# Turning tiles with both halves of TensorE's rows at once, two tensors to a pair of banks

## The chip, the cores and the metric

The kernel runs on one core of a Trainium2 chip. The metric is the device time of one execution in microseconds (us), the median of three executions: 617.34 us before the change (617.13 to 621.12).

## What is computed

Two blocks follow each other. The first is a linear recurrence over 768 tokens for 4 batches of 8 heads of width 40; the second is an MLP with a softmax-weighted activation and a layer norm.

```python
# r, k, v, w, a, b: (4, 8, 768, 40) float32
for t in range(S):
    y[:, :, t] = np.einsum('bhd,bhde->bhe', rt, state)
    Sa = np.einsum('bhde,bhe->bhd', state, at)
    state_decay = state * wt[:, :, None, :] - np.einsum('bhd,bhe->bhde', Sa, bt)
    state = state_decay + np.einsum('bhd,bhe->bhde', vt, kt)
# x = y as (3072, 320); w_in (320, 1024), w_out (1024, 320), g_ln (1024,), float64 in DRAM
h = x @ w_in
solu = h * softmax(h)
ln = (solu - mean(solu)) / np.sqrt(var(solu) + 1e-06) * g_ln
out = (ln @ w_out).astype(np.float32)
```

## The kernel before

The tokens are cut into 12 chunks of C = 64, and two batches share the 128 partitions: batch 0 of a pair in partitions 0 to 63, batch 1 in 64 to 127. That makes N = 24 units of work (2 batch pairs x 12 chunks). Within a chunk the recurrence is solved with small matrix products and the inverse of a 64x64 triangular matrix per head, so most products need the chunk's tensors with head width in the partitions and tokens along the free axis. The raw data lie the other way round (tokens in partitions), so each is turned by TensorE: `turned` (L347) takes a tensor of 128 partitions (two batches of 64 tokens) and 8 heads of 64 columns, and makes four transposes of 128 rows by 104 columns (two heads at a time), each into a quarter of one bank of PSUM. A copy of ScalarE (`kept`, L357) or a product on VectorE takes the bank into SBUF. Per unit these are turned: `ei` (the decay, L362, evicted into `ex`), `a` (`front`, L368, evicted by VectorE as `aT`), `b` (`front_b`, L376), `k` and `v` (`attend_kv`, L493), `r` (`attend_r`, L500), and the carried state `st` (`stated`, L505, evicted as `s`). In the MLP, `folded` (L711) turns the 128x1024 activation `e` with eight full 128x128 transposes, four to a bank, evicted as `lnT`.

The main loop (L823 to L901) is written out by hand: every engine runs its instructions in the order in which the program issues them. One pass of the loop is called a slot here. Slot i solves unit i of the recurrence, prepares units i+1 and i+2, runs the early steps for unit j = i + 5, and runs the MLP for units some three to four slots behind (m = i - 1; `hidden` L661, `highest`, `exped`, `weighed`, `folded`, `output` L723). `some` and `narrow` insert steps of two other lists on VectorE: the inversion of triangular blocks (`invert`, L423, 31 small steps per two units) and the conversion of the 64-bit weights.

PSUM has eight banks here: `ps1` is two buffers of a pair of banks (the small products rotate through them), `ps2` is one pair for the 128x1024 `h`, and `ps3` is two buffers of a single bank (`bank`, L142). All transposes, the cumulative sum of the decay (`pcum`, L333) and the output accumulator (`po`, L729) rotate through those two single banks.

TensorE is used with three shapes of the array. The small products use quarters (64 rows by 64 columns; four run at once, in four corners). The large products and the transposes use the full array. The third piece of the contraction of `h` has 64 rows only, and its two halves (L667 to L671, kt = 2) use the array's upper and lower half of rows, 64 rows by 128 columns each, each half writing its own bank; `fence` (L269) drains TensorE after it.

Of the kernel before, what the change touches and what calls it, by code (L numbers as in the profile page):

```python
# [17 lines left out]
P = 128  # L18
# [6 lines left out]
LAG = 1  # L25


THIN = (5, 15)
LN_EXP = "natural_log_exp_and_others"


# [20 lines left out]
def kernel(  # L52
# [33 lines left out]
    dram = ctx.enter_context(tc.tile_pool(name="dram", bufs=3, space=bass.MemoryType.DRAM))  # L86
    ps1 = ctx.enter_context(tc.tile_pool(name="ps1", bufs=2, space=PSUM))
    ps2 = ctx.enter_context(tc.tile_pool(name="ps2", bufs=1, space=PSUM))
    ps3 = ctx.enter_context(tc.tile_pool(name="ps3", bufs=2, space=PSUM))
    ctx.enter_context(tc.manual_schedule(engines={mybir.EngineType.PE, mybir.EngineType.Pool, mybir.EngineType.DVE,  # L90
                                                 mybir.EngineType.SP, mybir.EngineType.Activation}))

# [46 lines left out]
    def banks(name):  # L139
        return ps1.tile([P, 2, 512], FP32, tag="banks", name=name)  # L140

    def bank(name):  # L142
        return ps3.tile([P, 512], FP32, tag="bank", name=name)

# [71 lines left out]
                land(LANDS_NEXT[load], nc.gpsimd)  # L218

    def turn_g():  # L220
        pg = bank("pg")
        nc.tensor.transpose(out=pg[:, 0:NF], in_=g_rows, identity=ident[0:NF, 0:NF])
        for x, y in zip(g_cols, (0, -20, -36)):
            nc.scalar.mul(out=x, in_=pg[:, 0:NF], mul=2.0 ** y)
# [4 lines left out]
            nc.tensor.matmul(t[:, 0:DM], lhsT=c_("mean"), rhs=w2[:, c, :], start=start and c == lo, stop=stop and c == hi - 1)  # L229

    def mean_of(lo, hi, begun):
        t = bank("pmean")
        nc.tensor.matmul(t[:, 0:DM], lhsT=ident, rhs=begun, start=True, stop=False)
        mean_part(t, lo, hi, False)
        return mean_kept(t)
# [55 lines left out]
    def ok(i):  # L291
        return 0 <= i < N
# [29 lines left out]
    def logged(i):  # L322
        lw = st[i]["lw"] = two.tile([P, DM], FP32, tag="lw", name="lw", bufs=1)
        nc.scalar.activation(out=lw, in_=st[i]["raw_w"].rearrange("p h d -> p (h d)"), func=AF.Ln)

    def decay(i):
        if not ok(i):
            return
        d = st[i]
        if "lw" not in d:  # L330
            logged(i)
        t = (bank("pcum") if i > 5 else ps2.tile([P, DFF], FP32, tag="h", name="h"))[:, 0:DM]
        nc.tensor.matmul(t, lhsT=c_("cum"), rhs=d["lw"], start=True, stop=True)  # L333
        nc.scalar.activation(out=ei_t[0][:, :, 0:D], in_=heads(t), func=AF.Exp)
        inv = d["inv"] = two.tile([P, DM], FP32, tag="inv", name="inv", bufs=4)
        nc.scalar.activation(out=inv, in_=t, func=AF.Exp, scale=-1.0)
# [7 lines left out]
            j = H * (n == "b")  # L344
            nc.gpsimd.tensor_tensor(out=kb[:, j:j + H, 0:D], in0=d["raw_" + n], in1=heads(d["inv"]), op=ALU.mult)

    def turned(name, x):  # L347
        t = bank("p" + name)
        for j in range(4):
            nc.tensor.transpose(out=t[0:W2, j * P:(j + 1) * P],  # L350
                                in_=x[:, 2 * j:2 * j + 2].rearrange("p a b -> p (a b)")[:, 0:W2], identity=ident)
        return t[0:W2].rearrange("p (j b t) -> p b j t", j=4, b=2)

    def tokens(name, bufs=1):
        return two.tile([P, 2, 4, C], FP32, tag=name, name=name, bufs=bufs)
# [1 line left out]
    def kept(name, t, bufs=1):  # L357
        o = tokens(name, bufs)
        nc.scalar.copy(out=o[0:W2], in_=t)
        return o  # L360

    def decay_turned(i):  # L362
        if not ok(i):
            return
        ex = st[i]["ex"] = ex_t[i % (AHEAD + 2)]
        nc.scalar.copy(out=ex[0:W2, :, :, 1:], in_=turned("ei", ei_t[0]))

    def front(i):  # L368
        if not ok(i):
            return  # L370
        d = st[i]
        t = turned("a", d["raw_a"])
        aT = d["aT"] = tokens("aT", AHEAD)
        nc.vector.tensor_tensor(out=aT[0:W2], in0=t, in1=d["ex"][0:W2, :, :, 0:C], op=ALU.mult)

    def front_b(i):  # L376
        if not ok(i):
            return
        d = st[i]
        d["bT"] = kept("bT", turned("b", d["kb"][:, H:]))  # L380

    def masked(dst, t):
        nc.vector.tensor_tensor(out=dst, in0=t.rearrange("p b (j c) -> p b j c", j=4),  # L383
# [109 lines left out]
    def attend_kv(i):  # L493
        if not ok(i):
            return
        d = st[i]
        d["kT"] = kept("kT", turned("k", d["kb"]))
        d["vT"] = kept("vT", turned("v", v_t[0]))

    def attend_r(i):  # L500
        if not ok(i):
            return
        st[i]["rT"] = kept("rT", turned("r", r_t[0]), 2)

    def stated(i):  # L505
        if not ok(i):
            return
        d = st[i]
        bp, ci = where_(i)
        if ci:  # L510
            t = bank("pst")
            for x in range(4):
                nc.tensor.transpose(out=t[0:W2, x * P:(x + 1) * P],  # L513
                                    in_=st_t[bp][:, 2 * x:2 * x + 2].rearrange("p a b -> p (a b)")[:, 0:W2], identity=ident)
            d["s"] = two.tile([P, 4, P], FP32, tag="s", name="s", bufs=1)
            nc.scalar.copy(out=d["s"][0:W2], in_=t[0:W2].rearrange("p (x t) -> p x t", x=4))

    def scores(i):
        if not ok(i):
# [141 lines left out]
    def hidden(i, some):  # L661

        if not ok(i):
            return
        d = st[i]
        for kt, x in some:
            if (kt, x) == (NK - 1, 0):  # L667
                d["h"] = ps2.tile([P, DFF], FP32, tag="h", name="h")
            part = slice(0, P) if kt < 2 else half(x)
            mm(d["h"][:, 512 * x:512 * x + 512], d["xT"][part, kt], w_in[part, 2 * kt + (x if kt < 2 else 0)],  # L670
               start=kt == NK - 1, stop=kt == NK - 2)  # L671
# [39 lines left out]
    def folded(i):  # L711
        if not ok(i):
            return
        d = st[i]
        lnT = d["lnT"] = two.tile([P, NF, P], FP32, tag="lnT", name="lnT", bufs=1)
        for x in range(2):
            t = bank("plnT")
            for j in range(NF // 2):
                f = x * (NF // 2) + j
                nc.tensor.transpose(out=t[:, j * P:(j + 1) * P], in_=d["e"][:, f * P:(f + 1) * P], identity=ident)  # L720
            nc.scalar.copy(out=lnT[:, x * (NF // 2):(x + 1) * (NF // 2)].rearrange("p f t -> p (f t)"), in_=t)  # L721

    def output(i, x):  # L723
        if not ok(i):
            return
        d = st[i]
        bp, ci = where_(i)
        if x == 0:
            d["out"] = bank("po")  # L729
        for f in range(x * NF // 2, x * NF // 2 + NF // 2):  # L730
            nc.tensor.matmul(d["out"][:, 0:DM], lhsT=d["lnT"][:, f, :], rhs=w2[:, f, :], start=f == 0, stop=f == NF - 1)  # L731
        if x == 0:
            return
        osb = two.tile([P, DM], FP32, tag="osb", name="osb", bufs=1)
        nc.scalar.activation(out=osb, in_=d["out"][:, 0:DM], func=AF.Copy, scale=d["rs"])  # L735
        nc.scalar.dma_start(out=out.rearrange("(b s) n -> b s n", b=B)[2 * bp:2 * bp + 2, ci * C:ci * C + C], in_=osb)
# [26 lines left out]
    load_keys(2, "ba")  # L763
    decay(0)
    logged(1)
    decay_turned(0)
    for i in range(4):
        if i != 2:
            scaled(i, "b")
        if i == 3:  # L770
            scaled(0, "k")
            scaled(1, "k")
        front(i)
        front_b(i)
        decay(i + 1)
        if i == 0:
            logged(i + 2)
        some(4 * (i > 2))
        norm(i)
        decay_turned(i + 1)  # L780
        if i == 1:
            load_keys(3, "w")
            scaled(2, "b")
            begin_inverse(0)
            narrow(2)
            load_keys(3, "ba")
            load_keys(0, "k")
            load_keys(4, "w")
            load_values(0)
            load_keys(1, "k")  # L790
            load_keys(4, "ba")
            load_keys(5, "w")
            land(2, nc.sync)
        if i == 2:
            some(12)
# [27 lines left out]
    for i in range(-1, N + 3 + LAG):  # L823
# [7 lines left out]
        narrow(0, pieces[0])  # L831

        solved(i)
        if i in THIN:
            stated(i)
            front(j)
        if i >= 0:
            scores(i + 1)
        if i >= 0:
            load_keys(j + 3, "w")  # L840
        load_keys(j + 2, "bak")

        if i not in THIN:
            stated(i)
            front(j)
        hidden(m - 2, ((0, 1),))
        if i == 3 + LAG:
            centred(mean)
        narrow(some_weights[1], pieces[1])
        front_b(j)  # L850
        if ok(j + 2):
            logged(j + 2)
        if i == 1 + LAG:
            first = ps2.tile([P, DFF], FP32, tag="h", name="mean")
            mean_part(first, 0, 2, True, False)
        decay_turned(j + 1)
        hidden(m - 2, ((1, 1),))
        flip(i + 1)
        highest(m - 2)
        scaled(j + 1)  # L860
        left(i - 1)
        if i == 1 + LAG:
            mean_part(first, 2, 3, False)
            mean = mean_kept(first)
        decay(j + 2)
        output(m - 3, 0)

        some(pieces[2])
        if i == 2 + LAG:
            mean = mean_of(3, 6, mean)  # L870
        couple(i + 1)
        exped(m - 2)
        norm(j)
        answered(i)
# [10 lines left out]
        carried(i + 1)  # L885
        narrow(some_weights[2], pieces[3], ok(j) and j % GRP == GRP - 1)
        by_value(i + 2)
        if ok(m - 1):
            hidden(m - 1, ((2, 0), (2, 1)))
        fence()  # L890
        read(i, False)
        driven(i + 1)
        leave(i)
        begin_narrow(narrowed.get(i + 1, (0,))[0])
        folded(m - 2)
        hidden(m - 1, ((0, 0),))
        attend_kv(i + 2)
        hidden(m - 1, ((1, 0),))
        attend_r(i + 2)
        if i == 2 + LAG:  # L900
# [31 lines left out]
```

## Time and profile before

| | us |
|---|---|
| three executions | 617.34, 617.13, 621.12 |
| the profiled execution, first to last instruction | 616.2 |
| TensorE busy (matmul) | 552.0 (90%) |
| VectorE busy | 449.0 (73%) |
| ScalarE busy | 265.8 (43%) |
| GpSimd busy | 258.0 (42%) |
| granted TensorE clock, mean | 0.928 |

All times below are from this one execution. The profile names an instruction by engine, line, operation and tiles (output <- inputs; for a matmul the moving operand first, then the stationary one). "128*104 128x128" is a matmul with 128 rows and 104 columns of weights and an output (for a transpose: a moving operand) of 128 columns. An ordinary float32 matmul leaves two records, a transpose one. Matmuls are pipelined: a record lasts from its start to the modelled end of its last row, so the time that a group takes on TensorE is read from the start of the group to the start of the next one, not from the sum of the records.

### The profile page before, as it was taken

Reading aid. Unit: us, or ns where it says so; the run is one execution under the profiler, and the core shown is the slowest. Engines: PE = TensorE matmul, PEld = TensorE weight load, DVE = VectorE, ACT = ScalarE, POOL = GpSimd, SP = SyncE. Lnnn points to the kernel's source line nnn. Section 1 sums busy time; section 2 is a strip of 40 time slices with the busy share of each in tenths; the row PEclk is TensorE's granted clock in tenths of the full one; section 3 lists DMA queues with packets and bytes.
Section 4 is the critical chain, followed back from the end, with each engine's and each line's share of the span. In section 5 each row is a group of like instructions: output and inputs, shape, how many; then the busy total and the mean of one; then the engine's idle time right before and its main releaser. Section 6 shows DMA issues by size and latency. Waiting matters only on the chain.

```text
span 616.2 us, 26656 instructions
## 1 busy us (share of the span) xinstructions
PE 552.0 (90%) x11453; PEld 401.9 (65%) x11453; DVE 449.0 (73%) x1262; ACT 265.8 (43%) x548; POOL 258.0 (42%) x424
## 2 busy tenths in 40 slices
PE   5555668889999999999999999999999999999994
PEld 3333457666676777777777777777777676676652
DVE  4797986988968869869868868788697588443431
ACT  3433444654543544454444445444433343342221
POOL 3463264283453472473365355444624631322200
PEclk9665765789999999999999999999999999999998
DMA  7986887476455455564564474564532622310100
GB/s 164 159 156 121 183 157 129 98 156 104 76 106 104 90 115 99 93 122 95 100 123 91 95 126 98 112 113 82 110 56 53 118 49 43 65 35 26 28 19 21
DMA packets 213901, 59.93 MB, mean 97 GB/s; under 512 B 199120, under 2 KB 208952, under 8 KB 213784
## 3 DMA queue, kind: packets, MB, share of 16 engines
q1 hardware_dynamic: 195512, 33.78, 32.8%
q0 software_dynamic: 11568, 19.78, 14.0%
q10 hardware_dynamic: 6704, 4.67, 2.7%
q8 instruction: 90, 1.47, 1.0%
q14 instruction: 27, 0.22, 0.1%
HBM read 40.10 MB, written 13.37 MB: 87 GB/s over the span
## 4 chain that ended last, share of the span: by engine, by line
PE 74%; DVE 17%; ACT 3%; issue 3%; DMA 1%; ACTq 1%; DVEq 0%; SPq 0%
PE po L731 16%; PE h L265 16%; PE pyo L265 8%; DVE uu L438 5%; DVE prod L436 5%; PE pu L265 4%; PE plnT L720 4%; PE ps L265 4%; PE px L265 3%; PE py L265 2%; PE pl L265 2%; PE pz L265 2%; PE pr L350 2%; PE pst L513 2%; PE pcum L333 1%
## 5 line engine op out<-in xcount | busy, mean ns | idle before, releaser
L265 PE MATMUL h<-w_in,xT 128*128 128x512 f32 (+1 forms) x288 | 123.7, 614 | 0.0
L731 PE MATMUL po<-w,lnT 128*128 128x320 f32 x384 | 112.7, 438 | 0.5 <-ACT lnT L721 0.5
L438 DVE TENSOR_TENSOR uu<-uu,prod 128x30 f32<-128x30 f32 (+4 forms) x360 | 102.1, 284 | 12.4
L436 DVE TENSOR_TENSOR prod<-blk,uu 128x30 f32<-128x30 f32 (+4 forms) x360 | 99.2, 276 | 9.6
L731 PEld LDWEIGHTS po<-w,lnT 128*128 128x128 f32 x384 | 71.0, 190 | 32.6 <-issue 4.1
L409 POOL DMA_DIRECT2D nt_dram<-nt x20 | 18.8, 938 | 120.8 <-DVE nt L383 99.8
L709 POOL TENSOR_TENSOR rs<-c,mhalf 128x1 f32<-128x1 f32 x24 | 13.5, 561 | 112.3 <-DVE c L708 103.4
L383 DVE TENSOR_TENSOR psi<-ps,cst 128x512 f32<-128x512 f32 x24 | 16.6, 690 | 59.5 <-PE ps L265 59.5
L658 POOL DMA_DIRECT2D xT<-x x96 | 48.9, 514 | 0.4 <-DMA blk<-nt_dram 0.3
L265 PEld LDWEIGHTS h<-w_in,xT 128*128 128x128 f32 (+1 forms) x288 | 37.6, 190 | 9.4 <-issue 8.1
L678 DVE TENSOR_REDUCE nmax<-h 128x1 f32<-128x1024 f32 x24 | 28.6, 1193 | 18.6 <-PE h L265 18.6
L420 POOL DMA_DIRECT2D blk<-nt_dram x46 | 36.9, 808 | 11.8 <-issue 8.4
L265 PE MATMUL pyo<-lv,kb 64*64 64x104 f32 x768 | 38.3, 269 | 2.2
L265 PEld LDWEIGHTS pyo<-lv,kb 64*64 64x64 f32 x768 | 24.1, 142 | 21.2 <-issue 21.1
L265 PE MATMUL pyo<-lu,kb 64*64 64x104 f32 x768 | 37.4, 262 | 0.1
L646 POOL TENSOR_TENSOR st<-tot,ex 104x160 f32<-104x160 f32 x44 | 21.7, 511 | 36.4 <-DVE tot L642 32.4
L562 ACT COPY x<-px 128x320 f32<-128x320 f32 x24 | 10.2, 426 | 56.3 <-PE px L265 56.1
L477 ACT ACTIVATE wy<-py,cst 128x256 f32<-128x256 f32 x24 | 11.4, 474 | 53.2 <-PE py L265 53.2
L288 POOL DMA_DIRECT2D raw_r<-in_r_dram x48 | 33.9, 709 | 0.0
L735 ACT ACTIVATE osb<-po,rs 128x320 f32<-128x320 f32 x24 | 12.7, 527 | 48.5 <-PE po L731 32.8
L686 ACT ACTIVATE e<-h,nmax 128x1024 f32<-128x1024 f32 x24 | 26.6, 1108 | 14.3 <-DVE nmax L678 14.3
L692 DVE TENSOR_TENSOR e<-h,e 128x1024 f32<-128x1024 f32 x24 | 29.2, 1217 | 4.7 <-ACT e L686 4.7
(131 smaller groups left out, 1169.1 us busy)
## 6 DMA issues: line engine op xcount, KB each, us to landing
blk<-nt_dram POOLq DMA_DIRECT2D x46, 128.0 KB, 4.7
nt_dram<-nt POOLq DMA_DIRECT2D x20, 256.0 KB, 3.7
raw_w<-in_w_dram SPq DMA_DIRECT2D x48, 80.0 KB
a<-in_a_dram SPq DMA_DIRECT2D x48, 80.0 KB
raw_r<-in_r_dram POOLq DMA_DIRECT2D x48, 80.0 KB, 3.6
lv<-in_v_dram SPq DMA_DIRECT2D x48, 80.0 KB
out_dram<-osb ACTq DMA_DIRECT2D x24, 160.0 KB
raw_b<-in_b_dram SPq DMA_DIRECT2D x44, 80.0 KB
```

Of the source, the lines that this page charges most:

```text
L265: nc.tensor.matmul(o, lhsT=lhsT, rhs=rhs, start=start, stop=stop, skip_group_check=True)
L288: queue.dma_start(out=x[half(p), :, 0:D], in_=ap[2 * bp + p, :, ci * C:(ci + 1) * C, :].rearrange("h t d -> t h d"))
L420: queue.dma_start(out=nb[home:home + Q], in_=blocks[n][:, Q * e:Q * e + Q, Q * e:Q * e + Q])
L436: nc.vector.tensor_tensor(out=t, in0=nb[:, j:j + 1, j + 1:Q].to_broadcast([P, n_c, m]), in1=u[:, 0:n_c, j:j + 1].to_broadcast([P, n_c, m]) ...
L438: nc.vector.tensor_tensor(out=u[:, 0:n_c, j + 1:Q], in0=u[:, 0:n_c, j + 1:Q], in1=t, op=ALU.subtract)
L646: nc.gpsimd.tensor_tensor(out=to3(old), in0=to3(tot[0:W2]), in1=ex[:, :, 2 * q:2 * q + 2, C:].to_broadcast([W2, 2, 2, D]), op=ALU.mult)
L658: nc.gpsimd.dma_start(out=xT[to:to + Q, 2], in_=x[at + P - 3 * D:at + D, 2])
L678: nc.vector.tensor_reduce(out=nmax, in_=d["h"], axis=AX.X, op=ALU.max, negate=True)
L686: nc.scalar.activation(out=e, in_=d["h"], func=AF.Exp, bias=d["nmax"], accum_out=d["esum"])
L692: nc.vector.tensor_tensor(out=d["e"], in0=d["h"], in1=d["e"], op=ALU.mult)
L720: nc.tensor.transpose(out=t[:, j * P:(j + 1) * P], in_=d["e"][:, f * P:(f + 1) * P], identity=ident)
L731: nc.tensor.matmul(d["out"][:, 0:DM], lhsT=d["lnT"][:, f, :], rhs=w2[:, f, :], start=f == 0, stop=f == NF - 1)
```

## The change

The four transposes of 128 rows become eight of 64 rows: for each two heads, one transpose of the upper 64 partitions and one of the lower 64, next to each other in the order. Each takes 64 columns of the identity and writes 64 columns; upper halves go to the first bank of a pair, lower halves to the second. A turned tensor then takes half of both banks, and two tensors share a pair. `ps3` becomes one buffer of a pair of banks, `spare`; the quick succession of single banks becomes a succession of pairs: `st` with `a`, `b` with `ei`, `pcum` with the output accumulator, `lnT`, `k` with `v`, and `r` alone. In the prologue `ei` and `a` are turned into pairs of `ps1`. `turn_g` and the mean use half of a `spare`.

```diff
-    ps3 = ctx.enter_context(tc.tile_pool(name="ps3", bufs=2, space=PSUM))
+    ps3 = ctx.enter_context(tc.tile_pool(name="ps3", bufs=1, space=PSUM))
-    def bank(name):
-        return ps3.tile([P, 512], FP32, tag="bank", name=name)
+    def spare(name):
+        return ps3.tile([P, 2, 512], FP32, tag="spare", name=name)
...
-    def turned(name, x):
-        t = bank("p" + name)
+    def turned(t, y, x):
+        at = 256 * y
         for j in range(4):
-            nc.tensor.transpose(out=t[0:W2, j * P:(j + 1) * P],
-                                in_=x[:, 2 * j:2 * j + 2].rearrange("p a b -> p (a b)")[:, 0:W2], identity=ident)
-        return t[0:W2].rearrange("p (j b t) -> p b j t", j=4, b=2)
+            for p in range(2):
+                nc.tensor.transpose(out=t[0:W2, p, at + C * j:at + C * j + C],
+                                    in_=x[half(p), 2 * j:2 * j + 2].rearrange("p a b -> p (a b)")[:, 0:W2],
+                                    identity=ident[half(p), half(p)])
+        return t[0:W2, :, at:at + 256].rearrange("p b (j t) -> p b j t", j=4)
```

`decay(j + 2)` takes the second bank of `out_bank` for `pcum`, and `output(m - 3, 0)` of the same slot the first bank of the same pair for `po`. `folded` writes its sixteen half transposes into both banks and evicts them with two copies, as before.

```diff
-        for x in range(2):
-            t = bank("plnT")
-            for j in range(NF // 2):
-                f = x * (NF // 2) + j
-                nc.tensor.transpose(out=t[:, j * P:(j + 1) * P], in_=d["e"][:, f * P:(f + 1) * P], identity=ident)
+        t = spare("plnT")
+        for f in range(NF):
+            for p in range(2):
+                nc.tensor.transpose(out=t[:, p, f * C:f * C + C], in_=d["e"][half(p), f * P:(f + 1) * P],
+                                    identity=ident[half(p), half(p)])
```

In the slot, the two transposes of a pair stand together, and other steps move. `logged` (ScalarE's logarithm of `w`) goes ahead of the turning of `b`. The two `hidden` steps of unit m - 2, which stood apart, stand together. `flip` and `highest` go ahead of VectorE's inversion steps. `couple` (the product `py` and its eviction `wy`) goes ahead of `decay` and `output`. `folded` goes ahead of the fence, and the half-row `hidden` behind it.

```diff
-        if i not in THIN:
-            stated(i)
-            front(j)
+        if ok(i) or ok(j):
+            t = spare("pst")
+            for evict in [stated(i, t, 0), front(j, t, 1)]:
+                evict()
+        if ok(j + 2):
+            logged(j + 2)
         hidden(m - 2, ((0, 1),))
+        hidden(m - 2, ((1, 1),))
...
+        flip(i + 1)
+        highest(m - 2)
         narrow(some_weights[1], pieces[1])
-        front_b(j)
...
-        decay_turned(j + 1)
-        hidden(m - 2, ((1, 1),))
-        flip(i + 1)
-        highest(m - 2)
+        if ok(j) or ok(j + 1):
+            t = spare("pb")
+            for evict in [front_b(j, t, 0), decay_turned(j + 1, t, 1)]:
+                evict()
...
+        couple(i + 1)
         decay(j + 2)
         output(m - 3, 0)
         some(pieces[2])
-        couple(i + 1)
...
-        if ok(m - 1):
-            hidden(m - 1, ((2, 0), (2, 1)))
+        folded(m - 2)
         fence()
         read(i, False)
         driven(i + 1)
         leave(i)
         begin_narrow(narrowed.get(i + 1, (0,))[0])
-        folded(m - 2)
+        if ok(m - 1):
+            hidden(m - 1, ((2, 0), (2, 1)))
+        attend_kv(i + 2)
         hidden(m - 1, ((0, 0),))
-        attend_kv(i + 2)
         hidden(m - 1, ((1, 0),))
         attend_r(i + 2)
```

The slots named in `THIN` (5 and 15), in which `stated` and `front` ran ahead of `scores`, are dropped. The first stage of the mean of `w_out` takes three pieces at once instead of two and one.

## Prediction

> **What bounds the kernel now.** I read first how busy each engine is by stage.
>
> ```profile
> core 0: us, PE busy (x) PEld busy (x) DVE busy (x) ACT busy (x) POOL busy (x), PEclk, DMA share, GB/s
> 0.00:59.00 59.00, 29.77 (x282) 20.02 (x282) 41.82 (x120) 22.90 (x45) 25.65 (x44) 0.69 0.81 148
> 92.50:117.00 24.50, 22.53 (x546) 19.65 (x546) 19.37 (x61) 12.13 (x25) 10.49 (x17) 0.55 0.62 116
> 161.00:506.00 345.00, 340.51 (x7685) 250.03 (x7687) 270.93 (x785) 155.89 (x325) 162.78 (x267) 1.00 0.51 98
> 562.00:616.20 54.20, 45.76 (x340) 27.80 (x330) 18.48 (x35) 13.16 (x24) 6.17 (x12) 0.97 0.07 22
> ```
>
> From 161 to 506 us, sixteen slots, TensorE is busy 98.7% at the full granted clock. VectorE has 79%, about 17 us of a slot of 21.6, and waits for TensorE. So a slot lasts as long as TensorE's list, and what this list loses or gains passes through. Before 161 us the clock is lower and transfers and VectorE share the path; after 562 us few transposes are left. One slot in TensorE's order of time (292.1 to 313.6), from the timeline:
>
> ```profile
> 293.06 0.67 PE L265 MATMUL ps<-aT,kT 40*64 40x64 f32 x32
> 293.55 0.65 PE L265 MATMUL ps<-rT,vT 40*64 40x64 f32 x32
> 294.13 0.64 PE L513 MATMUL pst<-cst,st 128*104 128x128 f32 x4
> 294.61 0.60 PE L350 MATMUL pa<-cst,a 128*104 128x128 f32 x4
> 295.05 1.02 PE L265 MATMUL h<-w_in,xT 128*128 128x512 f32 x2
> ...
> 296.35 0.60 PE L350 MATMUL pei<-cst,ei 128*104 128x128 f32 x4
> 296.78 1.02 PE L265 MATMUL h<-w_in,xT 128*128 128x512 f32 x2
> ...
> 300.93 0.67 PE L265 MATMUL pnt<-aT,bT 40*64 40x64 f32 x32
> 301.71 0.69 PE L265 MATMUL pl<-rT,nuT 40*64 40x64 f32 x32
> 302.33 2.42 PE L731 MATMUL po<-w,lnT 128*128 128x320 f32 x8
> ...
> 306.43 0.68 PE L265 MATMUL px<-st,aT 40*64 40x40 f32 x32
> 307.03 1.13 PE L265 MATMUL h<-w_in,xT 64*128 64x512 f32 x4
> ```
>
> Starts give the prices. Four transposes take 0.435 us (pei to h, pa to h), 0.109 each. Four quarter products of 64 columns take 0.061 us together (32 records in 0.49 us). The last row shows the form that the change wants: two halves of rows at once. Its four records of 512 columns span 1.13 us. Two full records one behind the other span 1.02, each step 0.43, so four would span 1.88 (562 to 565 us has such a row). The halves overlap.
>
> **1. Streaming, taken away.** Seven tensors of 4 transposes and 8 of plnT are 36 x 0.109 = 3.92 us a slot. After, it is 36 pairs of halves, each with 64 columns. Not overlapped, a half costs half of 0.109, so a pair costs at least 0.0545 and at most 0.109. The nearest row, quarters with 64 columns, gives 0.061 for four at once; I take it: 2.20 us, a saving of 1.7 (bounds 0 and 1.96). [...]
>
> **2. Borders between shapes of the array, added.** A change of shape shows as a late start. ps to pst is 0.58 where the like group took 0.49, and pst takes 0.48 against 0.44: 0.13. po to py (298.20 to 300.44) is 2.24 where eight records take 2.15: 0.09. pl to po is 0.62 against 0.49 and po then 2.35, of which 0.09 is its own end: about 0.2. px to the half-row h is 0.60 against 0.49, and more inside: about 0.2. Before, a slot has 8 borders (the transposes share the full shape with h and po). In the new order it has 14: quarters, halves (pst), full (h), halves (pb), quarters (py), full, quarters, full, quarters, halves (plnT), quarters, halves (h, pkv), full (h), halves (pr), quarters. Six more at 0.15 are +0.9 us (bounds 0.09 and 0.21: 0.5 to 1.3). [...]
>
> **3. A wait taken away.** pnt to pl is 0.78 us for a group of 0.49: pl waits for wy, ScalarE's eviction of py, 0.06 us after its end. couple moves ahead of pcum and po, more than 2 us earlier, so wy is long done: -0.3.
>
> **4. A wait added.** ScalarE in the same slot:
>
> ```profile
> 296.55 0.59 ACT L359 COPY bT<-pb 104x512 f32<-104x512 f32 x1 [1.15 <-PE pb L350]
> 297.03 0.47 ACT L324 ACTIVATE lw<-raw_w 128x320 f32<-128x320 f32 x1
> 297.40 0.58 ACT L366 COPY ex<-pei 104x512 f32<-104x512 f32 x1
> ```
>
> With two single banks, pcum found a free one. With one pair, pcum and po must wait until bT and ex have both left it. The copy starts 0.20 us behind the next group's start on TensorE (296.55 against 296.35), copies follow at 0.48, ex takes 0.58, and 0.06 passes to TensorE: 1.32 us from the end of the pair. In the order of the changed kernel only the first copy waits for TensorE, so I take both as starting after the whole pair. In between TensorE has py: a border and 0.49, 0.59 us, and 0.1 of the border to pcum. The stall is 0.6 us (0.4 if bT starts with its own half, 0.9 if ScalarE is late by half a copy). Queued behind pcum are po, pnt, pl, so all of TensorE.
>
> **5. The other handings-on of the pair, costed at nothing.** aT: VectorE runs psi, lv, aT from 294.27 to 296.15, and pb comes behind 1.7 us of h: some 0.4 us to spare, beyond that it stalls one for one. po to plnT: osb (0.53 us) has 2.3 us of pz, pyo, px. lnT to pkv: two copies of 1.07 us against 2.6 us of pyo, px and h. pkv to pr: copies of 1.07 against 1.7 of h. pr to pst: pu and ps, 2.0 us. lw ahead of bT on ScalarE falls into the h stretch, where ScalarE waited 1.15 us. plnT earlier needs e: VectorE ended its product at 305.13, plnT now comes some 2.5 us earlier than 309.57, which leaves over 1 us. flip and nmax ahead of the inversion steps make VectorE wait a few tenths for h, out of its 4.5 us of idle time.
>
> **Sum of a full slot:** -1.7 + 0.9 - 0.3 + 0.6 = -0.5 us.
>
> **By stage.** Sixteen full slots: -8. From 59 to 161 us (33.5, 24.5, 20.4, 24.0 us): -1.5. In the slot of 92.5 TensorE is the bound at clock 0.55, so -1; the others are mostly VectorE's and transfers'. Prologue: the chain of waits runs through some eight groups of transposes, 4.8 us at half clock, but the next w lands at its own time (a wait until 22.9) and the inversion steps carry the rest: -0.5. From 506 to 562: only st, k, v, r and plnT are left: -1. In the last four slots po's second half is followed at once by plnT, which now needs po's own pair free: 0.20 + 0.53 + 0.06 = 0.8 us of waiting for osb, less 0.4 of faster plnT: +1.5. Together -9.5: span 606.7 from 616.2. The profiled execution lies 1.1 us below the median, so the forecast is 608 us.
>
> **Rivals.**
> A. *The gain is given back*: borders at 0.21 or pairs at 0.08 us bring the slot to about 0. Against it: the quarters run at the rate taken. For: a half loads 104 or 128 columns of weights, a quarter only 64. Time 612 to 623, middle 616.
> B. *Transposes in halves don't overlap.* Place: the 36 pairs of a slot; price: the whole 1.7 us, so the slot is +1.2 and sixteen slots +19, with the smaller stages 640 us. It decides when a pair takes more than 0.075 us, where saving (1.2) equals the added 0.9 + 0.6 - 0.3. Against: the half-row h overlaps. For: it is an ordinary product, and both halves of a transpose write the same 104 partitions at full rate.
> C. *The single pair stalls more than once a slot*: aT or e late, 0.6 us more at two places, slot +0.7, about 628. VectorE's idle time speaks against it.
> D. *Cheap borders*: 0.09 each, pairs at 0.0545: slot -1.1, 596 us.
>
> **Numbers.** About 1% (6 us) is what a measurement can tell here. Forecast 0.45 (its own range 601 to 613), A 0.22, B 0.14, C 0.11, D 0.08. Faster by over 1%: D and all but a little of the forecast, 0.50; within 1%: A and that rest, 0.25; slower: B and C, 0.25. The range 594 to 630 leaves out B and little else.
>
> **What would show it.** Starts of consecutive groups of 8 half transposes about 0.24 us apart (B: 0.44). From pst to h, from h to pb and from pr to pu a lateness of 0.1 to 0.2. pcum late by 0.6 us behind py, released by ex, and no gap ahead of pl. Slots of 21.0 to 21.1 us between 161 and 506. In the last slots plnT released by osb. The forecast is wrong if VectorE's idle time vanishes, if the granted clock leaves 1.00 after 161 us, or if pb or pkv waits for an eviction.

## The result and the profile after

| | before | after |
|---|---|---|
| median, us | 617.24 (4 executions, 616.22 to 621.12) | 659.67 (4, 657.19 to 665.56) |
| ratio | | 1.068, 95% interval 1.062 to 1.074 |
| profiled execution, its span | 616.2 | 658.3 |
| TensorE busy | 552.0 | 547.4 |
| VectorE busy | 449.0 | 453.2 |
| mean granted clock, as the profile gives it | 0.928 | 0.950 |

The kernel became slower by 42 us. The prediction was 608, with a range of 594 to 630. TensorE's work did shrink; the time between its work grew. The times of runs are medians, and the profiles of E1 and E5 below are of the slowest executions of these two kernels (651.08 and 640.56 us).

The two mean clocks can't be compared as they stand. The profile counts time ahead of its first clock record as full speed, and that record comes at 91.3 us in the changed kernel, at 11.9 us before. Yet all 192 records of pnt in the changed kernel between 12.0 and 81.6 us last 311 ns or more, which is what they last where the clock is recorded at 0.50 (105.3 to 106.1 us); at 1.00 they last 218 ns (210 to 482 us). So the changed kernel spent about its first 91 us at half clock, and its mean is about 0.88, that of before about 0.92 (estimates, with the time ahead of the first record at half). In the view below the 0.89 of the first stretch is too high for the same reason. The kernel before had 20 us at full clock between 11.9 and 91.3 us.

Three stretches, cut in both kernels at the start of slots 4 and 20, show where. Columns are the stretch and its length, then each engine's busy time, then TensorE's granted clock, the DMA share and the bandwidth:

```profile
core 0: us, PE busy (x) PEld busy (x) DVE busy (x) ACT busy (x) POOL busy (x), PEclk, DMA share, GB/s
0.00:171.90 171.90, 108.99 (x2352) 81.58 (x2352) 133.29 (x375) 74.97 (x156) 75.96 (x122) 0.89 0.71 132
171.90:539.80 367.90, 334.71 (x8223) 232.97 (x8222) 272.11 (x778) 154.95 (x324) 159.07 (x261) 0.98 0.47 91
539.80:658.30 118.50, 103.66 (x1742) 67.45 (x1740) 47.77 (x109) 35.12 (x68) 21.71 (x42) 0.95 0.14 33
```

Before, these stretches lasted 161.3, 344.3 and 110.6 us; so +10.6, +23.6 and +7.9. In the middle one TensorE was busy 339.8 of 344.3 us; now it is 334.7 of 367.9. Its idle time went from 4.5 to 33.2 us, and the clock, 1.00 before, is 0.98. Of the idle time 16.2 us are waits for the shared pair (of po for inv, and of pcum and po for ex), 7.7 us waits of py for tu, and 6.3 us halts of TensorE that no other engine caused (the last section returns to them). The slots differ. The quiet ones last 22.1 to 22.2 us (21.5 before). In three, of 26.6, 23.8 and 25.3 us, the clock falls to half. Of the six others between 22.6 and 23.6 us, five hold a halt of 0.3 to 1.3 us. First a quiet slot, in TensorE's order of time (315.99 to 325.4), to be read against the slot shown with the prediction. The program gives both banks of the pair the name of the second user, so pcum appears as the po with lw:

```profile
315.99 0.43 PE L359 MATMUL pst<-cst,st 64*104 64x64 f32 x8
316.26 0.39 PE L359 MATMUL pst<-cst,a 64*104 64x64 f32 x8
316.57 1.98 PE L264 MATMUL h<-w_in,xT 128*128 128x512 f32 x4
318.49 0.43 PE L359 MATMUL pb<-cst,kb 64*104 64x64 f32 x8
318.76 0.39 PE L359 MATMUL pb<-cst,ei 64*104 64x64 f32 x8
319.07 0.67 PE L264 MATMUL py<-tu,nt 64*64 64x32 f32 x32
320.31 0.81 PE L332 MATMUL po<-lw,cst 128*128 128x320 f32 x2 [0.57 <-ACT ex L378]
321.97 2.42 PE L750 MATMUL po<-w,lnT 128*128 128x320 f32 x8 [0.85 <-ACT inv L335]
324.32 0.69 PE L264 MATMUL pnt<-aT,bT 40*64 40x64 f32 x32
324.84 0.65 PE L264 MATMUL pl<-rT,nuT 40*64 40x64 f32 x32
```

Eight halves take 0.22 us, and 0.27 directly behind a group of another shape, where four full transposes took 0.435 (in single records, the pairs start 0.056 us apart and the partner follows within 0.004). pl follows pnt with no gap. pcum stalls, 1.24 us behind py's start instead of the 0.59 of an undisturbed group. And then po stalls as well, 1.66 us behind pcum. ScalarE in the same stretch shows what it waits for:

```profile
319.18 0.58 ACT L369 COPY bT<-pb 104x512 f32<-104x512 f32 x1 [1.54 <-PE pb L359]
319.67 0.59 ACT L378 COPY ex<-pb 104x512 f32<-104x512 f32 x1
320.14 0.49 ACT L493 ACTIVATE wy<-py,cst 128x256 f32<-128x256 f32 x1
321.15 0.44 ACT L333 ACTIVATE ei<-po 128x320 f32<-128x320 f32 x1 [0.52 <-PE po L332]
321.49 0.43 ACT L335 ACTIVATE inv<-po 128x320 f32<-128x320 f32 x1
```

`ei` and `inv` are read out of pcum's bank, and po starts in the other bank only when inv is done (321.92). Before the change pcum and po had buffers of their own.

Now a long slot, 25.28 us (514.5 to 539.8). One line of VectorE, two of TensorE, then windows around them with the columns of the first fence:

```profile
522.55 0.45 DVE L481 STREAM_TRANSPOSE tu<-tu 128x256 f32<-128x256 f32 x1 [4.18 <-DMA tu<-uu_dram]
523.14 1.08 PE L264 MATMUL py<-tu,nt 64*64 64x32 f32 x32 [3.82 <-DVE tu L481]
524.15 4.39 PE L750 MATMUL po<-w,lnT 128*128 128x320 f32 x8
```

```profile
514.50:521.30 6.80, 4.68 (x144) 3.10 (x140) 1.29 (x2) 2.09 (x4) 6.45 (x12) 1.00 0.98 164
521.30:528.10 6.80, 4.96 (x40) 3.50 (x40) 5.04 (x18) 1.57 (x3) 0.15 (x1) 0.50 0.25 42
528.10:534.90 6.80, 6.69 (x195) 5.07 (x197) 6.32 (x20) 1.91 (x5) 0.57 (x1) 1.00 0.04 10
```

`flip` (L481) needs `tu` back from DRAM. Its turn on VectorE came at 518.4 us, when the transfer that brings tu had not even been issued (519.0); before, in the same slot, it was issued at 489.1 and flip's turn came at 492.6. It stands ahead of the inversion steps now, so VectorE stands still for 4.18 us with those steps queued behind it, and py, po and all that follows on TensorE wait with it. The DMA engines are 98% busy in this window; whether that made the transfer later still was not tested. Then the clock is at half for 6.8 us: po's eight records take 4.39 us in place of 2.42. So a wait of 4 us costs more than its length. The waits summed over the whole execution (total us, times, longest):

```profile
PE py L264 <- DVE tu L481: 13.5, 9, 3.8
PE po L750 <- ACT inv L335: 11.1, 13, 0.9
PE po L332 <- ACT ex L378: 8.6, 12, 2.2
...
DVE tu L481 <- DMA tu<-uu_dram: 17.2, 11, 4.2
...
PE pst L359 <- issue: 4.6, 3, 1.9
...
PE ps L264 <- issue: 2.8, 4, 1.3
```

("issue" stands where the engine waited for nothing that the profile shows.) Before, py waited 3.9 us for tu (5 times), VectorE 0.8 (once), and po for inv not at all. From 141 to 600 us the clock is at half for 27.3 us; before it was not there between 131.4 and 612.7 us.

### The profile page after: what moved, and what is told of

It reads as the page before. It is cut to its first block, busy times and chain, and to the rows that moved or that the text cites. A ratio compares the mean times of both kernels' runs of the same rounds, so it can differ in the third digit from the quotient of the medians.

```text
span 658.3 us, 28382 instructions
## 1 busy us (share of the span) xinstructions
PE 547.4 (83%) x12309; PEld 382.0 (58%) x12309; DVE 453.2 (69%) x1262; ACT 265.0 (40%) x548; POOL 256.7 (39%) x424
## 3 DMA queue, kind: packets, MB, share of 16 engines
q0 software_dynamic: 11568, 19.78, 13.3%
## 4 chain that ended last, share of the span: by engine, by line
PE 42%; DVE 27%; DMA 15%; issue 6%; SPq 5%; ACT 3%; POOL 1%; DVEq 0%; POOLq 0%; ACTq 0%
PE po L750 12%; PE h L264 11%; DVE prod L452 7%; DVE uu L454 7%; DMA uu_dram<-uu 6%; DMA tu<-uu_dram 5%; PE pyo L264 4%; PE pu L264 2%; DVE bs L716 2%; PE ps L264 2%; PE px L264 2%; DMA w<-in_moe_w_in_dram 2%; DVE e L708 2%; PE plnT L735 2%; DVE nmax L694 1%
## 5 line engine op out<-in xcount | busy, mean ns | idle before, releaser
L750 PE MATMUL po<-w,lnT 128*128 128x320 f32 x384 | 123.4, 469 | 12.9 <-ACT inv L335 11.1
L454 DVE TENSOR_TENSOR uu<-uu,prod 128x30 f32<-128x30 f32 (+4 forms) x360 | 100.0, 278 | 12.4
L452 DVE TENSOR_TENSOR prod<-blk,uu 128x30 f32<-128x30 f32 (+4 forms) x360 | 101.2, 281 | 10.3
L750 PEld LDWEIGHTS po<-w,lnT 128*128 128x128 f32 x384 | 74.2, 202 | 50.4 <-ACT inv L335 18.1
L725 POOL TENSOR_TENSOR rs<-c,mhalf 128x1 f32<-128x1 f32 x24 | 13.5, 562 | 120.2 <-DVE c L724 100.5
L264 PEld LDWEIGHTS h<-w_in,xT 128*128 128x128 f32 (+1 forms) x288 | 40.8, 189 | 32.8 <-issue 28.0
L662 POOL TENSOR_TENSOR st<-tot,ex 104x160 f32<-104x160 f32 x44 | 21.2, 498 | 36.8 <-DVE tot L658 29.8
L739 ACT COPY lnT<-plnT 128x512 f32<-128x512 f32 x48 | 25.8, 589 | 22.2 <-PE plnT L735 20.6
L716 DVE BATCH_NORM_STATS2 bs<-e 128x6 f32<-128x512 f32 x48 | 30.9, 685 | 0.8
L264 PE MATMUL py<-tu,nt 64*64 64x32 f32 x768 | 18.5, 240 | 13.5 <-DVE tu L481 13.5
```

The lines of the kernel that those rows point to most:

```text
L264: nc.tensor.matmul(o, lhsT=lhsT, rhs=rhs, start=start, stop=stop, skip_group_check=True)
L452: nc.vector.tensor_tensor(out=t, in0=nb[:, j:j + 1, j + 1:Q].to_broadcast([P, n_c, m]), in1=u[:, 0:n_c, j:j + 1].to_broadcast([P, n_c, m]) ...
L454: nc.vector.tensor_tensor(out=u[:, 0:n_c, j + 1:Q], in0=u[:, 0:n_c, j + 1:Q], in1=t, op=ALU.subtract)
L716: nc.vector.bn_stats(out=bs[:, x], in_=d["e"][:, x * 512:x * 512 + 512])
L739: nc.scalar.copy(out=lnT[:, fs].rearrange("q f (p t) -> q p f t", p=2), in_=t.rearrange("q p (f t) -> q p f t", f=NF)[:, :, fs])
```

## Experiments

The theory had three parts: (a) two tensors in one pair share their waits, so that po waits for the neighbour bank's copies; (b) the steps moved ahead wait for tu's way through DRAM; (c) every such hole in TensorE's work also lowers the clock. The rivals were that the halves themselves cost the time, and that the order of the transposes on TensorE (borders between shapes) does.

**E1. pcum in a pair of its own** (in `ps1`); everything else as in the changed kernel.

```diff
-        t = (out_bank(i)[:, 1] if i > 5 else ps2.tile([P, DFF], FP32, tag="h", name="h"))[:, 0:DM]
+        t = (banks("pcum")[:, 0] if i > 5 else ps2.tile([P, DFF], FP32, tag="h", name="h"))[:, 0:DM]
```

> The changed kernel with one edit: pcum goes into a pair of ps1, so the output accumulator has its pair alone. Theory (pair): in the changed kernel po begins 1.66 us behind pcum where before it was 0.55, released by ScalarE's copy inv out of the other bank of its own pair, and pcum itself waits 0.6 us for ex; 1.1 + 0.6 us in each of some 18 slots. Without it quiet slots fall from 22.1 to about 20.6 us and the time to 625 to 635 us; the waits of TensorE for tu stay. Rival (halves): the loss is in the half transposes and their borders; then the slots stay at 22 us and the time within 650 to 665 us.

Measured 645.07 us, 1.043 (1.035 to 1.051) of the kernel before: 15 us less than the changed kernel, and 10 us above what was expected. Both waits, of pcum for ex and of po for inv, are gone, so (a) is real. It isn't the whole: py, which now comes upon tu sooner, waits for it 22.7 us (14 times) instead of 13.5. A part of what was saved went into the next wait.

**E2. The moved steps back in their old places** (flip, highest and couple; the second `hidden` stays where the change has it), pcum still in the shared pair.

```diff
+        narrow(some_weights[1], pieces[1])
         flip(i + 1)
         highest(m - 2)
-        narrow(some_weights[1], pieces[1])
...
-        couple(i + 1)
         decay(j + 2)
...
+        couple(i + 1)
         exped(m - 2)
```

> The changed kernel with flip and highest again behind VectorE's inversion steps and couple (py) again behind the first half of po. Theory: the round trip of the inverse through DRAM, which these steps used to cover, accounts for the 13.5 us that TensorE waits for tu and for most of the 31 us at half clock behind 141 us (some 12 to 15 us lost); both go away. Against that, py no longer covers the wait of pcum for ex (+0.6 us a slot) and pl waits for wy again (+0.3), some 16 us. Together 640 to 655 us, with no wait for tu over 1 us and the clock at 1.00 from about 160 us. Rival (the early flip costs nothing): only the 16 us show, 670 to 680 us.

Measured 657.45 us, 1.066 (1.061 to 1.071): just outside what was expected. Of the waits for tu 2.3 us are left (3 times). But couple's py had stood between the pair of b and ei and pcum; without it pcum waits for the whole of ex:

```profile
PE po L332 <- ACT ex L378: 22.2, 17, 2.6
PE po L750 <- ACT inv L335: 11.1, 13, 0.9
```

That is 33.3 us of waits for the shared pair, against 19.7 in the changed kernel. Between slots 4 and 20 the clock, expected at 1.00, is still at half for 17.1 us: it falls five times, each time behind a window of the clock's grid (last section) with all or most of these two waits (1.17 and 0.86 us in a slot) and none for tu. The two causes cover each other: curing one alone lets the other grow.

**E5. Both edits, E1's and E2's, together.** (The diffs are those above.)

> The changed kernel with both edits at once: pcum in a pair of ps1, and flip, highest and couple in their old places; the fourteen borders and the half transposes stay. Theory (two waits and the early steps are the loss): against the version with the old places alone a slot loses the wait of po for inv (1.1 us) and half of the wait for ex (0.6), so quiet slots fall from 22.9 to about 21.2 us and the time to 618 to 634 us, with no wait for tu. Rival (the loss is in the borders, which only the regrouped version reduced): 640 us or more.

Measured 635.67 us, 1.026 (1.021 to 1.029), just above what was expected, with quiet slots of 21.2 to 21.5 us. py still waits 8.4 us for tu, all but 0.5 of it ahead of slot 4. Between slots 4 and 20 the clock is at half for 17.1 us again, each time at a halt of TensorE of 1.5 to 2.2 us that no other engine caused. Both cures together bring 24 us of the 42. In this order of the steps E1's edit is worth 22 us (from E2), in the other 15.

**E3. Full rows in the changed kernel's order.** The same order, pairs and copies, but each tensor turned by transposes of 128 rows into one bank.

```diff
-        at = 256 * y
         for j in range(4):
-            for p in range(2):
-                nc.tensor.transpose(out=t[0:W2, p, at + C * j:at + C * j + C],
...
+            nc.tensor.transpose(out=t[0:W2, y, P * j:P * j + P],
+                                in_=x[:, 2 * j:2 * j + 2].rearrange("p a b -> p (a b)")[:, 0:W2], identity=ident)
```

> The changed kernel with every transpose again over all 128 rows, each tensor in one bank of its pair; order and buffers stay as changed. Theory (halves save 1.7 us of streaming a slot; 14 borders become 11, 0.45 us): a quiet slot grows from 22.1 to about 23.4 us and the time to 675 to 690 us. Rival (halves save nothing or cost): 640 to 662 us.

Measured 671.56 us, 1.088 (1.083 to 1.094): somewhat below what was expected, and 12 us slower than with halves. Its quiet slot lasts 23.41 us, the changed kernel's 22.08. So the halves are a gain, and the rival that they don't overlap has fallen.

**E6. The moved steps alone, on the kernel before**: the second `hidden`, `flip` and `highest` ahead of the inversion steps, `couple` ahead of `decay`; all transposes as they were.

```diff
         hidden(m - 2, ((0, 1),))
+        hidden(m - 2, ((1, 1),))
...
+        flip(i + 1)
+        highest(m - 2)
         narrow(some_weights[1], pieces[1])
...
+        couple(i + 1)
         decay(j + 2)
```

> The kernel before, with full transposes and single banks, and only flip, highest and the second hidden moved ahead of the inversion steps, and couple ahead of pcum, as the change has them. Theory (the moved steps run into the round trip of the inverse through DRAM): TensorE waits for tu for 8 to 23 us in all, further windows at half clock behind 150 us, 627 to 645 us. Rival (the early steps only show where the slot is disturbed otherwise): no more than 5 us of waiting for tu, 612 to 622 us.

Measured 642.29 us, 1.039 (1.036 to 1.042): the moves alone cost 24 us. Quiet slots keep 21.59 us; the two longest, with the clock at half, take about 26. VectorE's and TensorE's rows of the waits:

```profile
DVE tu L465 <- DMA tu<-uu_dram: 21.8, 14, 3.7
...
PE py L265 <- DVE tu L465: 12.9, 9, 3.4
```

That is part (b) without any half transpose and without a shared pair. What else the new order costs in these 24 us was not parted from it.

**E10. As E6, but `couple` in its old place**, to part flip from couple (E6's diff without its last added line).

> The kernel before with flip, highest and the second hidden moved ahead of the inversion steps, and couple left in its old place. Theory (VectorE's order alone meets the round trip of the inverse; py behind the first half of po covers part of it): TensorE waits for tu for 2 to 6 us instead of 12.9, VectorE's wait for the transfer of tu stays near the 17 us of the changed kernel, 620 to 632 us. Rival (only couple's early place does it): 615 to 619 us.

Measured 643.47 us, 1.040 (1.038 to 1.042), well above what was expected. VectorE waits for tu as expected, TensorE for only 0.9 us, yet nothing is gained, for a cause that the edit brought in:

```profile
PE pcum L333 <- ACT lw L324: 19.8, 17, 6.1
...
DVE tu L465 <- DMA tu<-uu_dram: 17.6, 12, 3.6
```

The second h, moved ahead, had covered the logarithm lw; now only couple could, and it isn't there. So this run doesn't tell the two moves apart: how much of the 24 us flip alone costs stays open.

**E4. Regrouped.** Halves, with E5's cures, and the turnings put side by side: b with ei directly behind the pair of st and a, in a pair of `ps1`; r directly behind k and v, in `ps1` too. A slot then has 10 borders between shapes instead of 14.

```diff
+        if ok(j) or ok(j + 1):
+            t = banks("pb")
+            for evict in [front_b(j, t, 0), decay_turned(j + 1, t, 1)]:
+                evict()
...
         attend_kv(i + 2)
+        attend_r(i + 2)
         hidden(m - 1, ((0, 0),))
         hidden(m - 1, ((1, 0),))
-        attend_r(i + 2)
```

> A version built from the theory: transposes in halves; pcum, the pair of b and ei, and r in pairs of ps1; the pairs st/a and b/ei stand together, as do the half-row h, k/v and r (10 borders instead of 14); flip, highest and couple in their old places. Theory: streaming -1.7 and two more borders than before +0.3, no stall of pcum or po: slots of about 20.1 to 20.4 us against 21.55 before, 590 to 602 us. Rival (borders or halves dearer than read): 612 us or more.

Measured 617.57 us, 0.998 (0.994 to 1.001): quiet slots of 20.3 to 20.9 us, up to 0.5 us above what was expected, and the total 15 us above its upper end. Most of the missing time is in halts of TensorE that no semaphore explains, in the middle of a group. One of them, from the timeline:

```profile
264.86 0.63 PE L264 MATMUL px<-lv,psi 64*64 64x40 f32 x30
267.32 0.25 PE L264 MATMUL px<-lv,psi 64*64 64x40 f32 x2 [1.83 <-issue]
```

30 of 32 records run, and the last two come 1.83 us late; "issue" says that no other engine held them. This kernel has 13 such halts of 0.3 us or more, 13.4 us together, and the clock falls to half 0.7 us behind this one, for 3.4 us. At 264.81 a transfer of 16 KB of instructions had begun (the section on the hardware returns to it).

**E8. E4's order with full rows** (E3's edit in E4).

> The regrouped version with every transpose over all 128 rows. Theory (halves are worth 1.7 us less one border in each slot, and the halts of TensorE that no semaphore explains, 13.4 us in the regrouped version, come from twice as many transposes passing in half the time): quiet slots 21.8 to 22.0 us against 20.4, halts down to 3 us or less, together 626 to 638 us. Rival A (the halts have another cause): halts stay above 10 us, 638 to 650 us. Rival B (halves save nothing): 612 to 620 us.

Measured 628.96 us, 1.017 (1.014 to 1.019), as expected, quiet slots 21.74 us, no halt of 0.3 us. So halves are worth 11 us in this order too; the stretch from slot 4 to 20 tells what they bring and what they cost (E7, which follows, is E4 with a change in the last slots only). First E8, then E7:

```profile
166.60:512.90 346.30, 341.23 (x7659) 250.10 (x7658) 269.56 (x777) 154.82 (x325) 159.64 (x261) 1.00 0.50 97
```

```profile
166.90:504.60 337.70, 322.08 (x8223) 231.29 (x8222) 268.91 (x776) 153.88 (x325) 158.81 (x261) 0.99 0.52 99
```

TensorE's list shrinks by 19.2 us with halves, the stretch by 8.6: more than half of the gain is idle time again (15.6 us, of which 7.8 are halts, against 5.1).

**E7. E4 with lnT in a pair of `ps1` in the last four slots**, where plnT follows po's second half at once.

```diff
-        t = spare("plnT")
+        t = banks("plnT") if i >= N - 4 else spare("plnT")
```

> The regrouped version with the transposes of e (plnT) of the last four units in a pair of ps1 instead of the accumulator's own pair. Theory (in the last slots plnT waits 0.8 us for osb): the stretch behind the last pu falls from 57.1 to about 54.7 us, the time by 2 to 3 us, to 612 to 616 us. Rival: no change, 617 us.

Measured 613.63 us, 0.992 (0.989 to 0.995), as expected: the one version below the kernel before, by 0.8%, which is less than the 1% that the prediction took as measurable, though the interval excludes 1. From slot 23 to the end it takes 54.9 us, E4 57.1. Its quiet slots last 20.6 us; the same stretch of a slot as above:

```profile
358.32 0.43 PE L359 MATMUL pst<-cst,st 64*104 64x64 f32 x8
358.58 0.39 PE L359 MATMUL pst<-cst,a 64*104 64x64 f32 x8
358.81 0.39 PE L359 MATMUL pb<-cst,kb 64*104 64x64 f32 x8
359.03 0.39 PE L359 MATMUL pb<-cst,ei 64*104 64x64 f32 x8
359.35 1.98 PE L264 MATMUL h<-w_in,xT 128*128 128x512 f32 x4
361.17 0.70 PE L332 MATMUL pcum<-lw,cst 128*128 128x320 f32 x2
361.71 2.32 PE L750 MATMUL po<-w,lnT 128*128 128x320 f32 x8
363.95 0.67 PE L264 MATMUL py<-tu,nt 64*64 64x32 f32 x32
```

No row has a wait, h, pcum and po share one shape, and po follows pcum after 0.54 us instead of 1.66.

**E9. E7 with the two `hidden` steps ahead of the four turnings**, to see whether spreading the short instructions lessens the halts.

```diff
+        hidden(m - 2, ((0, 1),))
+        hidden(m - 2, ((1, 1),))
         if ok(i) or ok(j):
...
             logged(j + 2)
-        hidden(m - 2, ((0, 1),))
-        hidden(m - 2, ((1, 1),))
```

> The regrouped version with its tail edit, and the two h products of the other unit moved between ps and the run of half transposes st, a, b, ei, so that the burst of small instructions of pu and ps (256) is parted from the next burst by 1.7 us of two long products; one more border in the slot. Theory (TensorE uses up its instructions faster than they are fetched; every halt ended 2.2 to 3.4 us behind the start of a 16 KB fetch): halts fall from 10 to 13 us to 3 to 6 us, the border costs 0.15 to 0.2 us in each of 18 slots (3 us), together 606 to 613 us. Rival (the halts come from the half transposes themselves): halts stay at 10 us or more, 614 to 619 us.

Measured 639.86 us, 1.035 (1.032 to 1.037). The halts do fall, to 5.4 us (10.0 in E7), but the total misses by far: h had covered the evictions and lw on ScalarE.

```profile
PE pcum L332 <- ACT lw L323: 25.4, 16, 1.8
...
DVE aT L386 <- ACT s L532: 29.9, 17, 2.3
```

**E11. E9 with `logged` ahead of those evictions.**

> The version with the h products between ps and the run of half transposes, with the one thing mended that held it up: ScalarE takes the logarithm lw ahead of the evictions s, bT and ex, since pcum waited for it for 25.4 us in 16 slots. Theory: this wait goes, the halts stay near 5 us, slots of about 20.6 us, 606 to 614 us. Rival (the late lw only hid a wait for s or ex of the same size): 622 us or more.

Measured 646.86 us, 1.048 (1.043 to 1.052). The wait for lw is gone, but aT still waits for s (30.1 us, 17 times), and po, flip and py are held behind it:

```profile
311.51 2.42 PE L750 MATMUL po<-w,lnT 128*128 128x320 f32 x8 [0.22 <-DVE aT L386]
...
314.98 0.67 PE L264 MATMUL py<-tu,nt 64*64 64x32 f32 x32 [1.05 <-DVE tu L481]
```

py waits for tu 14.3 us in all (15 times), and the halts are 11.5 us. TensorE's order is E9's, so the order alone did not lessen them there. The place of the h behind the turnings is needed as cover, whichever eviction goes first.

Not tried: fewer instructions with everything else equal, which would test the inference on the halts in the last section; and flip in its new place with tu's transfers started earlier.

## Why the prediction was wrong

*Steps 1 to 4 held.* A group of halves takes 0.22 us, 0.27 behind a border (0.24 was foretold). Borders cost 0.09 to 0.14 us where a group of halves is followed by another shape (0.15 was taken): pst to h 0.32 us, pkv to h 0.32, pr to pu 0.36, each against 0.22 of the group. The step from the half-row h to pkv, counted as no border, shows none: the eight halves behind it take 0.23 us (333.35 to 333.58). pl no longer waits. pcum stalls 0.65 us for ex (0.6).

*Step 5, "the other handings-on of the pair, costed at nothing", failed in what it left out.* It went through aT, osb, lnT, the pairs of k, v and r, and e; but not through the two copies ei and inv that leave pcum's half of a pair whose other half is po's. po stands directly behind pcum (0.56 us before), while inv ends 1.6 us behind pcum's start. That handing-on costs 1.66 - 0.56 = 1.1 us a slot, and the sum of -0.5 becomes +0.6; 22.07 to 22.08 us against 21.53 are measured. E1 takes this wait away. Over sixteen slots the sum so corrected makes +9 of the +23.6 us, where -8 was forecast (an estimate from the quiet slots).

*The same step priced flip ahead of the inversion steps at "a few tenths, for h".* It reckoned with h, which nmax reads, and not with tu, which flip reads. What came last was tu's way through DRAM, up to 4.2 us. For a slot in which it was in time (21.59 in E6) the price of nothing was right; but in some slots its transfer comes later than flip's new turn. The trace of before held a small warning: flip behind the inversion steps waited once, 0.8 us. The step was moved ahead of 3.0 us of VectorE work that had covered it (296.1 to 299.1 us in the slot shown with the prediction). E6 puts the price of the moves at 24 us, with no half transpose in the kernel.

*The assumption that the clock stays at 1.00 behind 161 us failed.* It was on the list of what would make the forecast wrong, but no price was given to it. Three of the sixteen slots have half clock; they are some 10 us longer together than quiet slots, with the waits for tu in two of them (an estimate from their lengths). In the long slot above the clock fell to half within a wait of 3.82 us. In a slot with no other wait it fell behind waits of 0.57 and 0.86 us, one behind the other (shown in the last section).

*A term was missing: halts of TensorE with no engine to blame.* The prediction has none. Between slots 4 and 20 they take 6.3 us, in the kernel before 1.1.

*VectorE's idle time did not vanish* (73.9 us of 344.3 before, 95.8 of 367.9 after), and pb and pkv wait for no eviction between 171.9 and 539.8 us. So these two signs did not come true.

*The smaller stages* were to give -1.5; they gave +18.5. Up to slot 4 some of it is the pair again: pr waits for vT 8.6 us (for kT 3.5 before), pb for aT 5.8 us; E7, where b, ei and r have pairs of `ps1`, reaches slot 4 at 166.9 us instead of 171.9. In the last slots plnT waits for osb 2.0 us in three slots, as was foretold, and E7's edit there saves 2.2. Slot 21 is 3.4 us longer than before; in it py waits 2.2 us for tu and the clock is at half for 3.4 us. The half clock of the first 91 us has no visible price: with full rows and an early rise of the clock slot 4 begins at 173.1 us (E3). The rest of these two stages was not taken apart.

*The rivals.* B (halves that don't overlap) had the nearest figure, 640, and the wrong mechanism: E3 and E8 both lose 11 to 12 us without the halves. C (the single pair stalls more often, 628) had the right kind of mechanism, but named aT and e; pb waited for aT only ahead of slot 4. No rival had steps moved into a wait for DRAM.

*What adds up.* From the changed kernel, curing both causes brings 24 us of 42 (E5), regrouping 18 more (E4, which changes borders, pairs and order at once, so that the borders' share stays open), the last slots 2 to 4 (E7: 2.2 within the profiles, 4 between the medians). The shares of the first two causes can't be given one by one, since each grows when the other is cured: the shared pair is worth 15 or 22 us, the moved steps 2 or 9, depending on which is cured first; on the kernel before, without a shared pair, they cost 24 (E6). The 17 us that E5 still lies above the kernel before were not parted into borders, halts and clock.

## What to carry to other kernels

When buffers are merged, list every reader of either half, and ask of each how soon behind it the other half's next writer stands; the shortest distance decides, not the largest transfer. A step that is moved ahead must be held against the arrival of its slowest input in the worst slot, since what stands behind it can wait with it: the inversion steps stood behind flip while VectorE waited 4.18 us in the long slot. Here work taken off the bound engine was worth less than its length: halves took 19.2 us off TensorE's list and 8.6 us off the stretch (E8, E7). A hole put in cost more: the wait of 3.82 us came with 6.8 us at half clock, in which po's eight records took 4.39 us in place of 2.42.

## What the runs showed of the hardware

**The clock fell behind windows with little work.** Changes of the granted clock lie on a grid of 3.413 us in all 13 traces: in that of the changed kernel it stays for 3.413, 6.827, 10.24, 20.48 us and longer whole multiples from one change to the next. A window here is the time from one point of this grid to the next. From 115 us on, windows at full clock were followed like this in the 13 traces together, by the share that TensorE was busy in them (its records, with their modelled ends):

| TensorE busy in the window | clock then fell to half | stayed |
|---|---|---|
| under 0.5 | 41 | 7 |
| 0.5 to 0.6 | 21 | 30 |
| 0.6 to 0.75 | 6 | 119 |
| over 0.75 | 0 | 1645 |

In the traces of the kernel before and the changed kernel alone the rows are 9 and 0, 1 and 4, 1 and 18, 0 and 257. The clock also fell behind short waits, in another slot (changed kernel, TensorE's timeline; at half from 412.11 to 415.52 us):

```profile
409.90 0.81 PE L332 MATMUL po<-lw,cst 128*128 128x320 f32 x2 [0.57 <-ACT ex L378]
411.56 4.11 PE L750 MATMUL po<-w,lnT 128*128 128x320 f32 x8 [0.86 <-ACT inv L335]
```

The two waits are those of the quiet slot, 1.43 us together, which leaves TensorE busy for 0.58 of a window that holds both. Here the eight records behind them took 4.11 us, in the quiet slot 2.42. This slot lasts 23.8 us (403.55 to 427.32, from pu to pu), the quiet ones 22.1; that it depends on whether both fall into one window of the grid is an inference from the table, not a run of its own.

**With halves the first clock record comes later.** The first clock record, at 1.00, comes at 10.5 to 14.4 us in the five kernels with full rows and at 66.6 to 96.3 us in the eight with halves; in the same order of steps at 13.3 against 66.6 (E8, E4) and 13.3 against 91.3 (E3, the changed kernel). Ahead of it pnt's records last 311 ns or more in all eight. Why it does so was not tested.

**Halts of TensorE follow transfers of instructions.** Halts of 0.3 us or more, with no semaphore to explain them: 0 to 2.8 us in the five kernels with full rows (before, E3, E6, E8, E10), 5.4 to 13.4 us in the eight with halves. In the same order of steps it is 0 against 13.4 (E8, E4) and 2.8 against 8.3 (E3, the changed kernel). All 79 halts end 2.20 to 3.42 us after a transfer of 16 KB began in one queue of instructions, one halt to one transfer. That queue has 97 transfers with halves and 90 with full rows; its row in the changed kernel's page (queue: transfers, MB, share):

```profile
q8 instruction: 97, 1.59, 1.0%
```

Its row before has 90 transfers and 1.47 MB, so the kernels differ little in their number. That the halts are waits for such transfers is an inference from these times, not tested by itself.
